# Softcap attention into a soft mixture of experts: queries and keys cast by transfers, and three exponential tiles per batch on VectorE rather than one

**Chip, cores, metric.** One Trainium2 chip, one core. The metric is device time of one execution in microseconds (us), median over runs. Executions of one kernel mostly agree within 0.3%; several kernels here, the old one among them, have now and then an execution about 2.5 us longer, which is told where it matters.

## The reference

```python
# q, k, v: (8 batches, 12 heads, 448 positions, 64); phi: (768, 32); w1: (8, 768, 1024); w2: (8, 1024, 768)
scores = q @ k.transpose(0, 1, 3, 2) / sqrt(64)
scores = cap * tanh(scores / cap)                  # cap = 30
attn = exp(scores - max) ; attn = attn / sum       # over keys
x = (attn @ v), heads put side by side             # (3584, 768)
logits = x @ phi
d = softmax of logits over the tokens ; slot_input = d.T @ x       # 8 experts x 4 slots
slot_out = relu(slot_input @ w1[e]) @ w2[e]
out = (softmax of logits over the slots) @ slot_out                # (3584, 768)
```

## The kernel before

Everything is scheduled by hand: the program fixes the order of each engine's instructions, and in the traces they run in that order (VectorE from 85.18 to 88.57 us of the changed kernel, below: key copy, last part of one tile, first part of the next, logit sum, as their slots put them). Attention works on 336 tiles of 128 x 448 scores, six to a **chunk**, so 56 chunks, seven to a batch of the input. "Chunk 2 of a batch" is one with number j%7 = 2. A **PV pass** multiplies the exponentials of two heads by their values on TensorE; VectorE then normalizes the result. The **logit sum** is the addition on VectorE that collects the logits of `x @ phi`. A **quad** is four heads, whose queries, keys or values are loaded together. PSUM holds the tiles that TensorE's matmuls and transposes write here (`space=PSUM` in the kernel). In the loop below each chunk has slots ("0", "a", "b", "c", "d") into which side work is hung with `at(chunk, slot, job)`.

```python
    exps = att.enter_context(tc.tile_pool(name="exps", bufs=4))   # four chunks of exponentials

    def tanh_chunk(i):                         # half a chunk: 3 tiles from PSUM, ScalarE
        j, half = divmod(i, CH // CS)
        if half == 0:
            exs[j] = exps.tile([P, CH, S], BF16, name="ex", tag="ex")
        # ... act.activation(exs[j][...], scores, ACT.Tanh, scale=...)

    def exp_chunk(j):                          # in place, ScalarE; tile 0 left out where VectorE does it
        exp_part(j, 1 if j in shared else 0, CH)

    shared = [j for j in range(NCH - 2) if j % 7 == 3 and j > 7] if cap < 80 else []

    def poly_exp(j, part):                     # one exponential tile on VectorE, in three parts
        t, bits = exs[j][:, 0, :], 2.0 ** 23
        if part == 0:    # three tensor_scalar: xe, xm, xe
            # ...
        elif part == 1:  # two scalar_tensor_tensor: xp <- xm ; xp <- xp, xm
            # ...
        else:            # two scalar_tensor_tensor: xp <- xp, xm ; t <- xp, xe
            # ...

    def cast(nm, Q):                           # a quad of heads, float32 -> bfloat16, VectorE
        t = cst.tile([P, NT, P], BF16, name=nm + "bf", tag=nm + "bf")
        dve.tensor_copy(t.rearrange("p c (h d) -> p h c d", h=2),
                        raws.pop((nm, Q)).rearrange("p h (c d) -> p h c d", d=DH))
        # ... then the load of the next quad

    def transp(nm, Q):                         # 7 transposes on TensorE, one copy on VectorE
        # ...
        for c in range(NT):
            pe.transpose(ps[:, c, :], src[:, c, :], ident)
        # ... dve.tensor_copy(t, ps)

    for j in range(NCH):                       # the loop; TensorE's order is the order of these lines
        run(j, "0")
        tanh_chunk(2 * j); tanh_chunk(2 * j + 1)
        # ... exp_chunk(j - 1)
        if pr is not None:
            pv_pass(pr, 0)                     # 14 matmuls, then norm(): reciprocal and xq on VectorE
        run(j, "a")
        qk_chunk(2 * j + 2)                    # scores of half of the next chunk
        run(j, "b")
        if pr is not None:
            pv_pass(pr, 1)
        run(j, "c")
        qk_chunk(2 * j + 3)
        run(j, "d")
```

Logit sums, transposes of attention output and of queries and keys share one bank of PSUM (tag "T"), so they follow each other in program order. The values are cast on GpSimd (`vcast`, two instructions per quad). `spare(n)` issues n matmuls without use, to keep TensorE busy.

The softmax here doesn't subtract the row's maximum and nothing guards it: scores larger than these inputs give would overflow.

## Time and profile before

| | before |
|---|---|
| median of the runs beside the changed kernel | 317.31 us (316.76 to 319.75, 4 runs) |
| span of the profiled run | 314.8 us |
| ScalarE / TensorE / VectorE / GpSimd busy | 89 / 86 / 62 / 34% |
| time from one batch to the next (start of the tanh of chunk 2 to the next such start) | 32.55 us, six times |
| last tanh of the attention | starts at 264.6 us; 50.3 us follow |

The lines of the page that carry these are in the prediction.

Waits of TensorE (engine, tile and line, what it waited for, us in total, times, longest):

```profile
PE sc L269 <- ACT ex L278: 7.9, 19, 0.7
PE qps L237 <- DVE lg L360: 2.7, 7, 0.4
```

TensorE waits for ScalarE (7.9 us), hardly for VectorE: the query transposes wait 0.4 us at most for the logit sum.

### The profile page before, as it was taken

The numbers are of one execution on the slowest core, as the hardware profiler recorded it, in microseconds if no ns is written. First come the engines' busy times: TensorE is split into PE (matmuls) and PEld (weight loads), VectorE is DVE, ScalarE is ACT, GpSimd is POOL, SyncE is SP. The second block draws the span as 40 slices with busy tenths as digits, with TensorE's granted clock in tenths as the row PEclk, the third lists the DMA queues.
The fourth block names the chain that finished last, engine by engine and source line by source line (L and its number), as shares of the span: only waits on it lengthen the run. The fifth ranks groups of instructions, "written<-read, shape, count | busy, mean of one in ns | idle before, by whom it ended". The sixth has DMA issues, their size and how long they took to land.

```text
span 314.8 us, 8844 instructions
## 1 busy us (share of the span) xinstructions
PE 269.4 (86%) x3804; PEld 191.0 (61%) x3804; DVE 193.7 (62%) x473; ACT 281.3 (89%) x208; POOL 106.5 (34%) x134
## 2 busy tenths in 40 slices
PE   7899898899889998898889989898889998998720
PEld 6667665667666665666666666666666677743400
DVE  3636565766586659575867587657766574327840
ACT  4999999999999999999999999999999999326730
POOL 2464342523543452354245416441732130200000
PEclk9999999999999999999999999999999999999985
DMA  8899999799999999999999999999999807898997
GB/s 223 267 234 238 291 244 269 159 231 256 235 210 231 266 237 207 254 220 266 194 225 269 221 264 190 242 235 266 209 232 254 214 14 207 290 393 301 389 411 314
DMA packets 57479, 77.68 MB, mean 247 GB/s; under 512 B 3809, under 2 KB 53601, under 8 KB 57441
## 3 DMA queue, kind: packets, MB, share of 16 engines
q0 software_dynamic: 30480, 25.22, 52.1%
q1 hardware_dynamic: 26672, 51.68, 48.1%
q8 instruction: 29, 0.48, 0.6%
q10 hardware_dynamic: 288, 0.23, 0.2%
q14 instruction: 10, 0.07, 0.1%
HBM read 91.32 MB, written 18.87 MB: 350 GB/s over the span
## 4 chain that ended last, share of the span: by engine, by line
ACT 67%; PE 20%; DVE 5%; issue 3%; DMA 2%; DVEq 0%; ACTq 0%
ACT ex L278 33%; ACT ex L282 32%; PE pv L318 5%; PE sc L269 3%; PE so_ps L676 2%; PE junk L506 2%; PE hp L649 2%; ACT ob L754 1%; PE op L702 1%; DMA kraw<-in_k_dram 1%; DVE xq L329 1%; PE op L745 1%; PE xps L344 1%; DMA out_dram<-obh 1%; DVE ob L752 1%
## 5 line engine op out<-in xcount | busy, mean ns | idle before, releaser
L278 ACT ACTIVATE ex<-sc 128x1344 bf16<-128x1344 f32 (+1 forms) x113 | 162.3, 1693 | 0.9 <-PE sc L269 0.8
L282 ACT ACTIVATE ex<-ex 128x2688 bf16<-128x2688 bf16 (+4 forms) x58 | 159.2, 2779 | 0.1
L318 PEld LDWEIGHTS <-ex 128*128 128x128 bf16 x1344 | 78.7, 97 | 21.5 <-DVE xq L329 17.8
L318 PE MATMUL pv<-vbd,ex 128*128 128x130 bf16 x1274 | 88.6, 220 | 2.6 <-ACT ex L282 0.7
L269 PE MATMUL sc<-qT,kT 64*64 64x448 bf16 x672 | 78.6, 358 | 8.2 <-ACT ex L278 7.9
L247 POOL CAST vbd<-vraw 64x896 bf16<-64x896 f32 x23 | 21.5, 936 | 103.6 <-PE pv L318 65.3
L269 PEld LDWEIGHTS <-kT 64*64 64x64 bf16 x672 | 27.3, 105 | 25.3 <-issue 7.5
L329 DVE TENSOR_TENSOR xq<-pv,rec 128x256 bf16<-128x256 f32 x91 | 38.6, 424 | 3.1
L328 DVE RECIPROCAL rec<-pv 128x4 f32<-128x4 f32 x91 | 16.5, 181 | 32.1 <-PE pv L318 31.2
L506 PEld LDWEIGHTS <-ones 128*128 128x128 bf16 x470 | 28.6, 100 | 11.6 <-DVE xq L329 8.0
L372 POOL COPY e<-E 128x512 bf16<-128x512 bf16 x9 | 7.2, 795 | 81.5 <-ACT E L366 49.6
L506 PE MATMUL junk<-ones 128*128 128x128 bf16 x433 | 31.4, 219 | 2.5 <-DVE xq L329 1.6
L239 DVE COPY kT<-kps 128x896 bf16<-128x896 bf16 x23 | 14.4, 625 | 24.6 <-PE kps L237 24.4
L109 POOL DMA_DIRECT2D w1b<-in_moe_w_dram x32 | 25.2, 791 | 0.0
L248 POOL CAST vbd<-vraw 64x896 bf16<-64x896 f32 x23 | 23.7, 1029 | 1.3
L346 DVE COPY xT<-xps 128x512 bf16<-128x512 bf16 x47 | 19.5, 415 | 3.2 <-PE xps L344 3.0
L344 PE MATMUL xps<-ident,xq 128*128 128x128 bf16 x188 | 18.1, 218 | 0.2 <-DVE zacc L383 0.2
L239 DVE COPY qT<-qps 128x896 bf16<-128x896 bf16 x23 | 14.2, 616 | 5.2 <-PE qps L237 5.2
L226 DVE CAST kbf<-kraw 128x896 bf16<-128x896 f32 x22 | 16.0, 728 | 1.3 <-DMA kraw<-in_k_dram 1.3
L237 PE MATMUL kps<-ident,kbf 128*128 128x128 bf16 x161 | 12.8, 219 | 4.2 <-DVE slacc L418 2.2
L237 PE MATMUL qps<-ident,qbf 128*128 128x128 bf16 x161 | 12.8, 219 | 3.2 <-DVE lg L360 2.7
L237 PEld LDWEIGHTS <-kbf 128*128 128x128 bf16 x161 | 10.0, 97 | 9.0 <-issue 8.3
(113 smaller groups left out, 255.5 us busy)
## 6 DMA issues: line engine op xcount, KB each, us to landing
w1b<-in_moe_w_dram POOLq DMA_DIRECT2D x32, 384.0 KB, 10.2
vraw<-in_v_dram SPq DMA_DIRECT2D x23, 448.0 KB, 6.6
qraw<-in_q_dram SPq DMA_DIRECT2D x22, 448.0 KB, 7.8
kraw<-in_k_dram SPq DMA_DIRECT2D x22, 448.0 KB, 6.0
w2d<-in_moe_w_dram POOLq DMA_DIRECT2D x20, 384.0 KB, 9.2
w2t<-w2d SPq DMA_DIRECT2D x20, 384.0 KB, 5.9
out_dram<-ob SPq DMA_DIRECT2D x8, 768.0 KB, 7.3
w2b<-in_moe_w_dram POOLq DMA_DIRECT2D x12, 384.0 KB, 9.9
```

The costliest lines, as they stand in the source:

```text
L109: pool.dma_start(out=w1b[e][:, js, fs], in_=w1r[:, e, js, fs])
L237: pe.transpose(ps[:, c, :], src[:, c, :], ident)
L239: dve.tensor_copy(t, ps)
L247: pool.tensor_copy(t[0:HP, :, :, 0:DH], raw[0:HP])
L248: pool.tensor_copy(t[HP:P, :, :, DH + 1:VW - 1], raw[HP:P])
L269: pe.matmul(sc[cs, u, 0:S], qkT["k", Q][r, c, cs], qkT["q", Q][r, :, cs], start=True, stop=True)
L278: act.activation(exs[j][:, half * CS + u0:half * CS + u1, :], sc[:, u0:u1, 0:S], ACT.Tanh, scale=qk_scale / cap)
L282: act.activation(exs[j][:, u0:u1, :], exs[j][:, u0:u1, :], ACT.Exp, scale=cap)
L318: pe.matmul(pvs[pr, half][:, n, 0:VW], exs[j][:, u, GOFF[g]:GOFF[g] + P], vbds[Q % 2][:, h, c, :], start=(c == 0 and n == 0), stop=(c == N ...
L329: dve.tensor_tensor(xq[Q][:, 2 * half:2 * half + 2, h * P:(h + 1) * P] .rearrange("p g (i d) -> p g i d", i=2), pv[:, :, :, 0:DH], rec.to_ ...
L344: pe.transpose(ps[:, g, :], xq[Q][:, g, h * P:(h + 1) * P], ident)
L506: pe.matmul(junk if home is None else home, ones, ones, start=True, stop=True)
```

## The change

Intent: ScalarE sets the pace, so give two more exponential tiles per batch to VectorE (chunks 1, 2 and 3 of a batch rather than 3 alone), and make room on VectorE by letting transfers do the casts of queries and keys. The keys and queries then lie head by head, so each transpose becomes a pair of 64-column ones; the keys of one quad are transposed a chunk earlier. The core of the diff:

```diff
-            sp.dma_start(out=t, in_=quad_ap(nm, Q))
+            (sp if nm == "v" else pool).dma_start(out=t, in_=quad_ap(nm, Q))   # bfloat16 tile: the transfer casts
...
         for c in range(NT):
-            pe.transpose(ps[:, c, :], src[:, c, :], ident)
+            for h in range(2):
+                pe.transpose(ps[h * HP:h * HP + HP, c, :], src[:, h, c * DH:(c + 1) * DH], ident)
...
-    shared = [j for j in range(NCH - 2) if j % 7 == 3 and j > 7] if cap < 80 else []
+    shared = [j for j in range(NCH - 2) if 1 <= j % 7 <= 3 and j > 7] if cap < 80 else []
...
-        quad_in(3 * b + 3, (j + 4, "a"), (j + 5, "a"), (j + 4, "d"), (j + 5, "c"),
+        quad_in(3 * b + 3, (j + 4, "a"), (j + 5, "a"), (j + 3, "d"), (j + 5, "c"),
...
-        at(j + 3, "d", spare, 10)
+        at(j + 3, "d", spare, 10 if b == 0 else 4)
...
-        for dj, slot, part in ((0, "a", 0), (0, "c", 1), (0, "d", 2)):
+        for part, (dj, slot) in enumerate((((0, "a"), (0, "c"), (1, "b")),
+                                           ((0, "c"), (0, "d"), (1, "a")),
+                                           ((0, "c"), (1, "a"), (1, "c")))[j % 7 - 1]):
             at(j + dj, slot, poly_exp, j, part)
```

Also in the diff: how the first two quads are still cast by engines, the slots in which the loads are issued, buffer bookkeeping, and the first output tile computed in two halves.

More of the change, by code (lines that the diff above doesn't have):

```diff
@@ L90 @@
     w1b = [wts.tile([P, NJ, F], BF16, name=f"w1b{e}", tag="w1", bufs=E)
-           for e in range(E - 1)]
+           for e in range(E - 2)]
     w2b = wts.tile([P, R2, D], BF16, name="w2b")
@@ L129 @@
     ld = att.enter_context(tc.tile_pool(name="ld", bufs=1))
-    cst = att.enter_context(tc.tile_pool(name="cst", bufs=1))
     ldv = att.enter_context(tc.tile_pool(name="ldv", bufs=1))
@@ L158, in raw_tile @@
     def raw_tile(nm):
-        return (ldv if nm == "v" else ld).tile([P, 2, S], F32, name=nm + "raw",
-                                               tag=nm + "raw")
+        if nm == "v":
+            return ldv.tile([P, 2, S], F32, name="vraw", tag="vraw")
+        return ld.tile([P, 2, S], BF16, name=nm + "b", tag=nm + "raw", bufs=2)
     def load(nm, Q):
@@ L164, in load @@
             t = raw_tile(nm)
-            sp.dma_start(out=t, in_=quad_ap(nm, Q))
+            (sp if nm == "v" else pool).dma_start(out=t, in_=quad_ap(nm, Q))
             raws[nm, Q] = t
     def load_first():
-        for nm in "qkv":
-            raws[nm, 0] = raw_tile(nm)
-        kc = raws["k", 0].rearrange("p h (c d) -> p h c d", d=DH)
+        for nm in "qk":
+            raws[nm, 0] = [ld.tile([P, S], F32, name=f"{nm}raw{h}", tag=nm + "raw", bufs=2)
+                           for h in range(2)]
+        raws["v", 0] = raw_tile("v")
+        kc = raws["k", 0][0].rearrange("p (c d) -> p c d", d=DH)
         kin = quad_ap("k", 0, 0).rearrange("p (c d) -> p c d", d=DH)
-        sp.dma_start(out=raws["q", 0][:, 0, :], in_=quad_ap("q", 0, 0))
+        sp.dma_start(out=raws["q", 0][0], in_=quad_ap("q", 0, 0))
         for c0, c1 in ((0, CS), (CS, NT)):
-            act.dma_start(out=kc[:, 0, c0:c1, :], in_=kin[:, c0:c1, :])
+            act.dma_start(out=kc[:, c0:c1, :], in_=kin[:, c0:c1, :])
         for nm in "kq":
-            sp.dma_start(out=raws[nm, 0][:, 1, :], in_=quad_ap(nm, 0, 1))
+            sp.dma_start(out=raws[nm, 0][1], in_=quad_ap(nm, 0, 1))
         t = wts.tile([P, 3, 2, S], F32, name="raw1", tag="w1", bufs=E)
+        t01 = wts.tile([P, 2, 2, NT, P], BF16, name="casts", tag="w1", bufs=E)
         for n, nm in enumerate("kqv"):
             raws[nm, 1] = t[:, n, :, :]
+            if nm != "v":
+                for Q in range(2):
+                    casts[nm, Q] = t01[:, n, Q, :, :]
             if nm == "v":
@@ L192, in first_pieces @@
                 copy(casts[nm, 0][:, c0:c1, cols],
-                     raws[nm, 0][:, h, c0 * DH:c1 * DH].rearrange("p (c d) -> p c d", d=DH))
+                     raws[nm, 0][h][:, c0 * DH:c1 * DH].rearrange("p (c d) -> p c d", d=DH))
             elif stage == "turn":
@@ L202, in first_half @@
             if h == 0:
-                casts[nm, 0] = cst.tile([P, NT, P], BF16, name=nm + "bf", tag=nm + "bf")
                 qkT[nm, 0] = qk.tile([P, NT, P], BF16, name=nm + "T", tag=nm + "T")
@@ L222, in first_half, with cast @@
                 load(nm, 2)
-    def cast(nm, Q):
-        t = cst.tile([P, NT, P], BF16, name=nm + "bf", tag=nm + "bf")
-        dve.tensor_copy(t.rearrange("p c (h d) -> p h c d", h=2),
-                        raws.pop((nm, Q)).rearrange("p h (c d) -> p h c d", d=DH))
-        casts[nm, Q] = t
-        if Q > 1:
-            load(nm, Q + 1)
+    def cast(nm):
+        dve.tensor_copy(casts[nm, 1].rearrange("p c (h d) -> p h c d", h=2),
+                        raws.pop((nm, 1)).rearrange("p h (c d) -> p h c d", d=DH))
     def transp(nm, Q):
-        src = casts.pop((nm, Q))
+        src = casts.pop((nm, Q)) if Q == 1 else raws.pop((nm, Q))
         home = (psV, "pv") if (nm, Q) == ("k", 1) else (psT, "T")
@@ L236, in transp @@
         for c in range(NT):
-            pe.transpose(ps[:, c, :], src[:, c, :], ident)
+            if Q == 1:
+                pe.transpose(ps[:, c, :], src[:, c, :], ident)
+                continue
+            for h in range(2):
+                pe.transpose(ps[h * HP:h * HP + HP, c, :], src[:, h, c * DH:(c + 1) * DH], ident)
         t = qk.tile([P, NT, P], BF16, name=nm + "T", tag=nm + "T")
@@ L441, in quad_in @@
         if 0 < Q < NQ:
-            at(*cast_k, cast, "k", Q)
-            at(*cast_q, cast, "q", Q)
+            for nm, when in (("k", cast_k), ("q", cast_q)):
+                at(*when, *((cast, nm) if Q == 1 else (load, nm, Q + 1)))
             at(*k_in, transp, "k", Q)
@@ L453 @@
             quad_in(3 * b + 1, (j - 1, "b"), (j, "a"), (j - 1, "d"), (j, "c"), (j + 1, "d"))
-        quad_in(3 * b + 2, (j + 1, "c"), (j + 2, "c"), (j + 2, "b"), (j + 2, "d"),
+        quad_in(3 * b + 2, (j, "d"), (j + 1, "c"), (j + 2, "b"), (j + 2, "d"),
                 (j + 4, "d"))
-        quad_in(3 * b + 3, (j + 4, "a"), (j + 5, "a"), (j + 4, "d"), (j + 5, "c"),
+        quad_in(3 * b + 3, (j + 4, "a"), (j + 5, "a"), (j + 3, "d"), (j + 5, "c"),
                 (j + 6, "d"))
@@ L701, in half_tile @@
         bb, c = divmod(n, NT)
+        if n == half == 0:
+            for p, (bank_p, mul) in enumerate(zip(home, (act.mul, dve.tensor_scalar_mul))):
+                cs = slice(p * HD // 2, (p + 1) * HD // 2)
+                pe.matmul(bank_p, et_tile(bb, c), so[half][:, cs], start=True, stop=True)
+                mul(ob[:, cs], bank_p, winv[:, bb, c:c + 1])
+            store(n, half, half + 1, ob)
+            return
         pe.matmul(home, et_tile(bb, c), so[half], start=True, stop=True)
@@ L721 @@
             for eng in ("act", "dve"):
-                half_tile(done, 0, bank([P, HD], name="op0"), eng)
+                half_tile(done, 0, bank([P, HD], name="op0") if done else
+                          [bank([P, HD // 2], name="op00") for _ in range(2)], eng)
                 done += 1
```

## The prediction

> **What bounds the kernel now.** I read the page's busy line and chain first, to name the limiting engine; then the chain in order of time, to price one tile; then the same chain in a late window, to see who stands right behind the limit; then busy times by chunk.
>
> ```profile
> PE 269.4 (86%) x3804; PEld 191.0 (61%) x3804; DVE 193.7 (62%) x473; ACT 281.3 (89%) x208; POOL 106.5 (34%) x134
> ACT 67%; PE 20%; DVE 5%; issue 3%; DMA 2%; DVEq 0%; ACTq 0%
> L278 ACT ACTIVATE ex<-sc 128x1344 bf16<-128x1344 f32 (+1 forms) x113 | 162.3, 1693 | 0.9 <-PE sc L269 0.8
> L282 ACT ACTIVATE ex<-ex 128x2688 bf16<-128x2688 bf16 (+4 forms) x58 | 159.2, 2779 | 0.1
> ```
>
> ScalarE is busy 89% of the span, has two thirds of the chain, and its tanh (L278) and exponential (L282) have 1.0 us of idle time ahead of them in all. From 6.8 to 266 us, the attention stage, it practically never waits. The rest, some 49 us, is layers and stores. The chain in order of time gives its beat:
>
> ```profile
> 52.02 2.36 ACT ex L278 x2
> 54.38 2.33 ACT ex L282
> 56.91 2.36 ACT ex L278 x2
> 59.27 1.96 ACT ex L282
> ```
>
> A chunk is 2.36 us of tanh and 2.33 us of exponential, 4.69 us. Where VectorE already takes one tile of six (chunk 10, whose exponential runs during chunk 11) the exponential is 1.96 us: **0.37 us saved per tile**. But the same view of 214 to 246 us leaves ScalarE at 216.6 and does not come back for a whole batch. It starts like this:
>
> ```profile
> 217.40 0.92 PE pv L318 x14
> ...
> 218.56 0.42 DVE xq L329
> 218.99 0.54 DVE xp L300
> ...
> 219.55 0.64 DVE xp L301
> ...
> 220.22 0.64 DVE xp L303
> ...
> 220.87 0.92 DVE ex L304
> ...
> 221.91 0.43 DVE xq L329
> ...
> 222.40 0.97 PE pv L318 x14
> ```
>
> The reader is to see that the one exponential tile on VectorE already stands on the chain: the second normalization (221.91) waits behind its four multiply-adds, and TensorE's next PV pass (222.40) waits for that normalization. TensorE and VectorE together form a second loop, nearly as long as ScalarE's. The busy times by chunk (chunks 16 to 19, columns PE, PEld, DVE, ACT, POOL) say why:
>
> ```profile
> 80.00:84.70 4.70, 3.84 (x57) 2.80 (x55) 2.15 (x4) 4.70 (x5) 3.47 (x5) 1.00 0.90 242
> 84.70:89.59 4.89, 4.32 (x62) 3.19 (x60) 4.17 (x11) 4.89 (x5) 0.00 (x0) 1.00 1.14 220
> 89.59:93.91 4.32, 3.63 (x63) 2.54 (x61) 3.46 (x9) 4.32 (x4) 2.71 (x4) 1.00 1.13 189
> 93.91:98.65 4.74, 4.32 (x58) 3.23 (x58) 3.46 (x9) 4.74 (x4) 3.19 (x4) 1.00 0.95 240
> ```
>
> In chunk 17, which has that tile, VectorE is busy 4.17 of 4.89 us. Chunk 16 is light, for it has no PV pass.
>
> [...] the last multiply-add (L304) takes 627 ns once and 911 to 915 six times, a GpSimd copy or cast beside it where I looked, and a cast of 0.62 us becomes 0.98 beside one. [...] The trace shows the kinds equally fast per source byte: 50.4 MB of weights, cast, took 52.1% of the engines, and 51.7 MB uncast took 48.1%. [...]
>
> **The change, part by part.**
> 1. *Exponential tiles.* The rule goes from j%7 = 3 (7 tiles) to 1, 2, 3 (21). 14 more leave ScalarE: 14 x 0.37 = **5.2 us off the path**, if all else keeps up. On VectorE a tile is 0.38+0.39+0.39+0.61+0.63+0.63+0.63 = 3.7 us without contention (groups by form), 14 x 3.7 = +52 us.
> 2. *Casts.* 44 of 46 whole-quad casts leave VectorE: 16.0+14.5 = -30.5 us. Net +21 us of 193.7; per batch of 32.7 us from 22.1 to about 25.5. It fits on average.
> 3. *Transposes.* 22 quads x 2 x 7 become pairs of 64-column ones, 308 more matmuls; 42 filler matmuls go (six per batch), and the instruction count agrees with both. 64-column transposes of one half took 0.55 us for 7 (at 7.85 us), as do whole ones. [...] I take 95 ns per pair against 79 (between fully side by side and in turn): 6 x 7 x 16 ns = +0.7 us per batch, less 6 fillers x 73 ns = 0.4. About nothing.
> 4. *GpSimd.* 44 more issues of 0.79 us, and it is 34% busy: off the path.
> 5. *Tail.* The first output tile is halved between two engines, so the first store goes some 0.2 us sooner.
> All of it at full worth: 317.2 - 5.2 - 0.2 = 311.8 us.
>
> **Where it may be given back.** The order of instructions puts the new parts on VectorE like this, from chunk 16 on: key copy, last part of tile 1, first part of tile 2, *logit sum*, query copy, second part of tile 2, *normalization*, and so on. TensorE must have the logit sum before it transposes the queries (one PSUM bank for both), and the PV pass of chunk 17 stands behind these transposes. With starts to starts from the timeline (key copy 0.54, last part 1.21, first part 1.18): key copy at 82.7 as before, logit sum at 85.6 instead of 83.95, query transposes at 86.0 instead of 84.30, PV at 86.6 instead of 84.69: 1.9 us later. The middle part (1.23) then delays the normalization to 88.5, the second PV pass to 89.2 instead of 86.62, and the second half of the scores to 90.7. ScalarE at its new pace asks for that half at 80.00 + 2 x 4.32 + 0.20 (the small exponential of the logits) + 1.18 = 90.0. So it stalls 0.7 us, and two tiles saved 0.74: a first batch breaks even here. Carried on in the same way through chunks 17 to 22, the next batch's first scores come 34.5 us after this batch's, against 32.7 now (81.24 to 113.97).
>
> **Rivals.**
> *A, ScalarE still sets the pace.* For it: casts leave the busiest time of VectorE, chunks 5, 6 and 0 of a batch get lighter, the parts are placed in the chunk without PV, and the scores are 2.2 to 2.9 us ahead of ScalarE in chunks 15 to 17. Gives 312 to 315.
> *B, the loop of TensorE and VectorE takes over.* For it: the late chain and the working above. At 1.8 us for each of six batches after the first, about +10 us: 327; with 0.5 us per batch instead, 320. Against it: some fifty steps, each uncertain by 0.03 us.
> *C, the keys and queries land late.* GpSimd is in order, so a load stands behind a value cast that waits for PV (65 us of such waits, up to 6.6 each).
>
> ```profile
> w1b<-in_moe_w_dram POOLq DMA_DIRECT2D x32, 384.0 KB, 10.2
> qraw<-in_q_dram SPq DMA_DIRECT2D x22, 448.0 KB, 7.8
> ```
>
> A GpSimd transfer lands after 10.2 us. The tightest load by my count, queries issued after the cast of 70 to 72 us and wanted in the slot at 84, has 11 us. It should just do; where it does not, some tenths per batch go. [...] 319 to 324.
>
> **Range and chances.** The floor is 311.8, so over 2% faster (310.9) needs a gain that I do not see: 0.05. I give A 0.4, centred on 313.5, and B and C together 0.6, centred near 324, since the loop was already at its limit before. The weighted mean is 0.4 x 313.5 + 0.6 x 324 = 319.8; I say **319.5 us**, range **312 to 330**. Slower by over 2% means above 323.6, somewhat over half of B and C: 0.35. Within 2%: 0.60.
>
> **What would show it.** Right for part 1: 21 exponentials of five tiles at 1.96 us in the chain, and L282 some 5 us less busy. Right for the casts: no whole-quad cast after quad 1, and VectorE some 20 us busier. For B: ScalarE waits for scores (0.8 us now) for several us in all, once or more per batch in chunks 3 to 5, the chain in the middle of the run passes through PV, normalization and polynomial, and the query copy waits some 2 us more per batch. For C: the transposes of keys or queries wait for a DMA. For A: ScalarE's waits stay under 2 us. I am wrong in the working if the normalization behind a polynomial part does not hold up PV, or if ScalarE waits although VectorE has idle time just there; wrong in the size if the 64-column transposes take turns, which would show as 14 of them in over 1 us.

## More of the kernel before

The slices of the page show TensorE's granted clock, each digit a fortieth of the span, 9 for (nearly) full.

```profile
PEclk9999999999999999999999999999999999999985
```

## The result, and the profile after

The changed kernel takes **345.64 us** (345.37 to 345.79, 4 runs) against 317.31 in the same rounds. The ratio is 1.0876, 95% interval 1.0819 to 1.0932. It is slower, and outside the predicted range. The page of the changed kernel (busy line, granted clock, chain by engine):

```profile
PE 286.1 (83%) x4071; PEld 198.2 (58%) x4071; DVE 222.5 (65%) x528; ACT 278.7 (81%) x208; POOL 139.7 (41%) x178
PEclk9999998999999978999999989995999859999965
PE 45%; DVE 33%; ACT 13%; DMA 3%; issue 2%; DVEq 0%; SPq 0%; ACTq 0%
```

Two things are to be seen. ScalarE's share of the chain fell from 67% to 13%, and VectorE's rose from 5% to 33%: the limit has changed hands. And TensorE's granted clock, full before, dips in several slices. (The dip in the last slices, the stores, was there before; the others are new.) The waits of the changed kernel:

```profile
ACT ex L286 <- PE pv L326: 26.0, 17, 3.6
PE qps L245 <- DVE lg L368: 13.5, 7, 1.9
PE pv L326 <- DVE ex L312: 8.3, 7, 1.3
```

ScalarE, which waited 0.8 us, now waits 26.0 us for the PV pass (a tanh needs one of the four buffers of exponentials, which a PV pass frees). TensorE waits 13.5 us for the logit sum, once per batch 1.9 us, where it was 2.7 us in all, and 8.3 us for the last polynomial part. The chain in order of time, in the middle of the run (start, length, what), shows where these waits come from:

```profile
84.63 0.53 PE kps L245 x14
...
85.18 0.62 DVE kT L247
85.81 0.55 DVE xp L311
86.37 0.64 DVE ex L312
...
87.11 0.40 DVE xe L302
...
87.96 0.40 DVE xe L306
88.36 0.21 DVE lg L368
...
88.61 0.60 PE qps L245 x14
...
97.74 0.80 DVE xp L311
...
98.57 1.26 DVE ex L312
...
99.88 0.52 PE pv L326 x6
```

Between the key copy and the logit sum stand the last part of tile 1 (L311, L312) and the first part of tile 2 (L302 to L306). TensorE, which must have that sum, transposes queries only at 88.61. Except for these transposes (until 89.23) VectorE is on the chain without a gap until 99.83, where the last part of tile 3 ends and a PV pass can go on. The timeline of the same stretch (start, length, engine, line, what, how often, and the idle time before it with its releaser):

```profile
88.61 0.58 PE L245 MATMUL qps<-ident,qb 128*64 128x128 bf16 x14 [1.94 <-DVE lg L368]
...
90.03 0.76 PE L277 MATMUL sc<-qT,kT 64*64 64x448 bf16 x6
...
91.65 0.98 PE L326 MATMUL pv<-vbd,ex 128*128 128x130 bf16 x14 [0.87 <-DVE xq L337]
...
92.55 2.47 ACT L286 ACTIVATE ex<-sc 128x1344 bf16<-128x1344 f32 x2 [1.85 <-PE pv L326]
```

TensorE stands still for 1.94 us, the second PV pass starts at 91.65, and ScalarE, ready at 90.70, starts the tanh at 92.55, though its scores had been there from 90.79.

**Where 29.2 us of span went** (314.8 to 344.0), from the starts of the tanh of chunk 2 in the traces, and the run with fillers below (e4), which has the change at full clock:

| part | before | with fillers, full clock | changed | 
|---|---|---|---|
| batch to batch, mean of six | 32.55 | 34.96 | 35.87 |
| chunk 2 of the last batch starts | 242.45 | 257.13 | 262.43 |
| from there to the last tanh | 22.10 | 25.62 | 28.75 |
| after the start of the last tanh | 50.28 | 52.86 | 52.81 |
| span | 314.84 | 335.60 | 343.99 |

So with the clock at full: 14.7 us in the batches before, 3.5 in the last one, 2.6 after it, 20.8 in all; the other 8.4 are the clock. (The profiled run before is one of its shortest, so the medians of the times differ by 28.3 rather than 29.2.)

The granted clock can be read directly in windows of 8 us (window, length, then busy us and instructions of PE, PEld, DVE, ACT, POOL, then the granted clock, the share of the DMA engines and GB/s). The changed kernel:

```profile
264.00:272.00 8.00, 6.01 (x102) 4.52 (x100) 5.72 (x12) 7.48 (x6) 1.72 (x3) 1.00 0.66 161
272.00:280.00 8.00, 7.25 (x57) 5.04 (x56) 4.75 (x12) 4.43 (x3) 0.79 (x1) 0.50 0.01 2
```

From 272 to 280 us TensorE runs at half clock: 57 matmuls keep it busy for 7.25 us, where 102 took 6.01 just before. The clock's records in the trace have six such stretches:

```text
start us   length us   granted clock
 53.62       3.41        0.5
125.30       6.83        0.5
196.97       3.41        0.5
231.11      10.24        0.5
272.07      10.24        0.5
330.10      15.91        0.5    (the stores; before: from 304.12)
```

The first five start after or in the 1.93 to 1.94 us in which TensorE waits for the logit sum (51.4, 121.9, 194.3, 229.6 and 268.6 us); after the same wait at 86.7 and 158.9 the clock stayed. Before the change TensorE had one idle stretch of over 0.7 us before 299 us, of 0.75 us. A single wait of that length wasn't needed: in e5 below the clock halved seven times before 335 us, and no idle stretch of TensorE up to there was over 1.37 us. And e4 kept its clock through the attention with stretches of up to 1.30 us. So the length of one wait did not decide it here; what did was not looked into.

### The profile page after: what moved, and what is told of

It is laid out like the page before. It is cut to its first block, busy times and chain, and to the rows that moved or that the text cites. A ratio compares the mean times of both kernels' runs of the same rounds, so it can differ in the third digit from the quotient of the medians. Undisturbed runs are those within 1.5% of the kernel's fastest.

```text
span 344.0 us, 9411 instructions
## 1 busy us (share of the span) xinstructions
PE 286.1 (83%) x4071; PEld 198.2 (58%) x4071; DVE 222.5 (65%) x528; ACT 278.7 (81%) x208; POOL 139.7 (41%) x178
## 4 chain that ended last, share of the span: by engine, by line
PE 45%; DVE 33%; ACT 13%; DMA 3%; issue 2%; DVEq 0%; SPq 0%; ACTq 0%
PE pv L326 16%; PE sc L277 9%; ACT ex L286 7%; DVE xq L337 6%; ACT ex L290 5%; DVE ex L312 4%; PE junk L516 4%; DVE xp L311 3%; DVE qT L247 3%; PE kps L245 3%; DVE xp L309 2%; DVE rec L336 2%; DMA out_dram<-ob 2%; PE xps L352 2%; DVE xm L304 2%
## 5 line engine op out<-in xcount | busy, mean ns | idle before, releaser
L286 ACT ACTIVATE ex<-sc 128x1344 bf16<-128x1344 f32 (+1 forms) x113 | 140.0, 1291 | 28.8 <-PE pv L326 26.0
L290 ACT ACTIVATE ex<-ex 128x2688 bf16<-128x2688 bf16 (+4 forms) x58 | 130.0, 2246 | 0.1
L326 PE MATMUL pv<-vbd,ex 128*128 128x130 bf16 x1274 | 96.7, 230 | 13.3 <-DVE ex L312 8.3
L326 PEld LDWEIGHTS <-ex 128*128 128x128 bf16 x1344 | 84.1, 102 | 37.5 <-DVE xq L337 20.3
L277 PE MATMUL sc<-qT,kT 64*64 64x448 bf16 x672 | 83.1, 376 | 1.5 <-ACT ex L286 1.2
L255 POOL CAST vbd<-vraw 64x896 bf16<-64x896 f32 x23 | 22.6, 983 | 104.6 <-PE pv L326 88.8
L256 POOL CAST vbd<-vraw 64x896 bf16<-64x896 f32 x23 | 25.9, 1126 | 1.3
L245 PE MATMUL qps<-ident,qb 128*64 128x128 bf16 x308 | 13.4, 228 | 13.6 <-DVE lg L368 13.5
L245 PEld LDWEIGHTS <-qb 128*64 128x64 bf16 x308 | 10.5, 112 | 15.4 <-issue 13.7
L352 PE MATMUL xps<-ident,xq 128*128 128x128 bf16 x188 | 18.6, 222 | 0.8 <-DVE kT L247 0.3
L309 DVE SCALAR_TENSOR_TENSOR xp<-xp,xm 128x448 f32<-128x448 f32 x21 | 18.4, 876 | 0.7
L312 DVE SCALAR_TENSOR_TENSOR ex<-xp,xe 128x448 bf16<-128x448 f32 x21 | 17.5, 835 | 0.7
```

The source lines that it names most:

```text
L245: pe.transpose(ps[h * HP:h * HP + HP, c, :], src[:, h, c * DH:(c + 1) * DH], ident)
L256: pool.tensor_copy(t[HP:P, :, :, DH + 1:VW - 1], raw[HP:P])
L277: pe.matmul(sc[cs, u, 0:S], qkT["k", Q][r, c, cs], qkT["q", Q][r, :, cs], start=True, stop=True)
L286: act.activation(exs[j][:, half * CS + u0:half * CS + u1, :], sc[:, u0:u1, 0:S], ACT.Tanh, scale=qk_scale / cap)
L290: act.activation(exs[j][:, u0:u1, :], exs[j][:, u0:u1, :], ACT.Exp, scale=cap)
L309: dve.scalar_tensor_tensor(xp, xp, POW2[2], xm, ALU.add, ALU.mult)
```

## The experiments

Each was compared with the kernel before in the same rounds. "Batches" are the six times from batch to batch as above. Theory: the loop of TensorE and VectorE sets the time, because of the amount of VectorE work put into chunks 1 to 3, and the clock adds to it. Rivals: late transfers, the order of the parts, GpSimd's casts slowing VectorE, the number of buffers.

### Casts by transfers alone, one tile (e1)

```diff
-    shared = [j for j in range(NCH - 2) if 1 <= j % 7 <= 3 and j > 7]
+    shared = [j for j in range(NCH - 2) if j % 7 in (3,) and j > 7]
     # and its parts in the old slots: (0, "a"), (0, "c"), (0, "d")
```

> The changed kernel with one exponential tile per batch on VectorE, in the chunk and the slots of the kernel before; everything else of the change stays (casts by transfers, paired transposes, key transposes sooner, fillers, tail). Theory 1 (the added VectorE work lengthens the loop of TensorE and VectorE): VectorE has some 4 us per batch less than in the kernel before, so ScalarE sets the pace again: 315 to 318 us, a batch takes 32.5 us as before, and the TensorE clock never falls in the attention stage. Theory 2 (loads and casts on GpSimd, or the doubled transposes, cost the time): it stays above 330 us, and transposes wait for DMAs.

Measured: 318.29 us (318.03 to 320.85), before 317.61; ratio 1.0037 (0.9972 to 1.0103). Batches 32.55, as before, clock full (0.976 to 0.982 over the runs, with the stores; before 0.98 to 0.986). So, while ScalarE sets the pace, neither the transfers nor GpSimd's issues nor the paired transposes cost anything that can be told from noise, and taking 28 us from VectorE (193.7 to 165.4 us busy) gains nothing by itself, since ScalarE still sets the pace. The transfers on the GpSimd queue of the changed kernel even landed sooner than weights, which are larger, did before (10.2 us for 384 KB; KB each, us from issue to landing):

```profile
qb<-in_q_dram POOLq DMA_DIRECT2D x22, 224.0 KB, 6.2
kb<-in_k_dram POOLq DMA_DIRECT2D x22, 224.0 KB, 7.7
```

and no transpose of keys or queries waited for a DMA, in e1 or in the changed kernel. The late loads of rival C are out.

### Three tiles without the new casts (e2)

```diff
     # the kernel before, with the three tiles per batch and the slots of the change
-    shared = [j for j in range(NCH - 2) if j % 7 == 3 and j > 7]
+    shared = [j for j in range(NCH - 2) if 1 <= j % 7 <= 3 and j > 7]
```

> The kernel before with the three tiles in the changed kernel's slots; queries and keys are still cast on VectorE. If VectorE's load in chunks 1 to 4 sets the loop, the casts that stay there (two key casts and one or two query casts of 0.62 us among them) make it longer than in the changed kernel: batches of 35.5 to 37 us and 346 to 360 us. If casts by transfers did not help the loop: 343 to 346 us.

Measured: 370.8 us (2 runs), ratio 1.1689; batches 37.61 to 41.13; mean clock 0.905 and 0.896 in the two runs; ScalarE waits 51.4 us for PV. More than expected. With three tiles the casts by transfers, with the rest of the change (key transposes a chunk earlier, fewer fillers), are worth 25 us; with one tile they are worth nothing. Here the worth of this part went with which engine set the pace.

### Two tiles (e9 and e8)

```diff
     # e9: tiles of chunks 1 and 3 in the slots of the change
-    shared = [... if 1 <= j % 7 <= 3 and j > 7]
+    shared = [... if j % 7 in (1, 3) and j > 7]
     # e8: the same tiles, tile 1 at (1, "a"), (1, "c"), (1, "d"), tile 3 in the old slots
```

> The changed kernel without its second tile: chunks 1 and 3 of a batch keep theirs, in the changed kernel's slots. If the amount of VectorE work sets the loop: 3.7 us less VectorE work between the key copy and the last part, so batches come to 32.2 to 33.5 us, the wait for the logit sum shrinks by 1.2 us to under 1 us, the clock stays full, and the whole is 316 to 324 us. If any tile next to the logit sum breaks it: batches stay above 34 us, above 335 us.

> Two tiles per batch: that of chunk 1 wholly in chunk 2, which has no PV pass (its last part behind the logit sum and the query copy), that of chunk 3 in the slots of the kernel before. If the loop of TensorE and VectorE has room there: batches of 32.2 us (32.55 less 0.37), 315.5 to 316.5 us. If it has none: batches of 32.6 us and more, 318 us and up.

Measured: e9 322.91 us (2 runs), ratio 1.0155, batches 32.18 to 33.37, clock full (0.98 over the profiled run), 4.0 us of waits for the logit sum. e8 325.56 us (4 runs), ratio 1.0254, batches 33.08 to 33.93: the PV pass waits for the tile's last part (7.8 us, 7 times), so those slots are too late, and the worse branch of the expectation came true. (Two of its four runs were 3 us longer at a clock of 0.959 rather than 0.98.) In the slots of the change one tile less takes the mean batch from 34.96 at full clock (e4) to 32.84 (e9), so the amount of work matters, and not in proportion: the slack is used up first. But it isn't the amount alone. The same two tiles in the slots of e10 below take 32.17, and in e8's 33.30.

### Fillers in TensorE's wait (e4)

```diff
+        if b:
+            at(j + 2, "d", spare, 22)          # 22 matmuls without use ahead of the query transposes
         quad_in(3 * b + 2, (j, "d"), (j + 1, "c"), (j + 2, "b"), (j + 2, "d"),
```

> The changed kernel with 22 filler matmuls (1.6 us) put where TensorE waits 1.9 us for the logit sum, in each of the seven batches. Theory 1b (these idle stretches halve TensorE's clock for 3.4 to 10.2 us, which stretches the batches of 37.6, 35.9 and 37.7 us): the clock stays at full until the stores, every batch takes 34.6 to 34.9 us, and the whole is 335 to 338 us. Rival (the low clock falls where TensorE waits for VectorE anyway): 344 to 347 us.

Measured: 337.34 us (336.55 to 337.43, 4 runs), ratio 1.0604. The granted clock of its page:

```profile
PEclk9999999999999999999999999999999999999975
```

The batches take 34.59, 34.62, 35.53, 34.86, 35.52 and 34.61 us. The second and the fourth, in which the changed kernel kept its clock too, took 34.65 and 34.87 there, so the fillers lie in idle time. (The first took 34.57 in spite of 3.4 us at half clock.) The clock is thus worth 345.64 - 337.34 = **8.3 us**, shown by adding work and nothing else. Two of the six took 0.9 us longer at full clock. The timeline shows 0.6 of it: in these batches the sums for the output weights (`e_sums`, every second batch) stand ahead of the logit sum in chunk 1, and all that follows on VectorE comes 0.60 us later. The rest stays open.

### GpSimd's value casts made tiny (e3, e7)

```diff
-        pool.tensor_copy(t[0:HP, :, :, 0:DH], raw[0:HP])
+        pool.tensor_copy(t[0:HP, :, 0:1, 0:1], raw[0:HP, :, 0:1, 0:1])
     # likewise the other half; the result is wrong on purpose
     # e7: the same and the fillers of e4
```

In the changed kernel's timeline the same two multiply-adds are seen beside GpSimd's cast and without it:

```profile
82.45 1.23 POOL L256 CAST vbd<-vraw 64x896 bf16<-64x896 f32 x1
...
82.90 1.26 DVE L309 SCALAR_TENSOR_TENSOR xp<-xp,xm 128x448 f32<-128x448 f32 x1
...
90.42 0.63 DVE L309 SCALAR_TENSOR_TENSOR xp<-xp,xm 128x448 f32<-128x448 f32 x1
```

1.26 us rather than 0.63. Such long ones come about once per batch at each of the four multiply-adds (0.80, 1.26, 0.80 to 1.00 and 1.25 us, rather than 0.62), some 1.7 us per batch.

> The changed kernel, but GpSimd's two value casts per quad write one column each; the result is wrong on purpose. Theory 1a (VectorE's two-input polynomial parts wait for GpSimd's casts, and that is on the path): the parts that take 0.80, 1.26, 0.88 and 1.25 us beside a value cast go back to 0.62, 1.7 us per batch, 7 batches: some 12 us less, 332 to 335 us, more if the clock recovers too. Rival (the contention lies where VectorE has slack): within 3 us of 345.6.

> The changed kernel with the 22 fillers and with the tiny value casts (wrong on purpose), so that the contention is measured at a steady clock. If VectorE's wait for GpSimd's casts is on the path: batches of 33.7 us, as those of the tiny-cast run that kept their clock, instead of 34.6 to 35.5 in the run with fillers alone, and 329 to 332 us. If the casts cost nothing on the path: 336 to 338 us.

Measured: e3 342.39 us (2 runs), ratio 1.0768: all but four of the 84 parts were back at 0.61 to 0.63 us and the undisturbed batches at 33.71, but the clock dropped in more batches (0.86 to 0.95 in four of six; 0.929 and 0.912 over the two runs), so the total missed its expectation and says nothing on the size. e7, with the clock held but for 3.4 us in the last batch, tells it: 331.84 us (2 runs), ratio 1.0436, batches 33.74 to 34.76, mean 34.14. Against e4 that is **5.5 us**, and 0.82 per batch: half of the 1.7 us summed from the durations reach the time. The trace shows where. Chunk 3 is as slow as in e4 (6.66 and 6.67 us), but chunks 5 and 6 take 4.69 and 4.67 rather than 5.04 and 5.07: the last part of tile 3 no longer stands beside a cast (0.62 + 0.63 us rather than 0.88 + 1.26), and the PV pass that waits for it starts sooner.

### Parts moved behind the logit sum and the query copy (e5)

```diff
-        (((0, "a"), (0, "c"), (1, "b")), ((0, "c"), (0, "d"), (1, "a")), ((0, "c"), (1, "a"), (1, "c")))
+        (((0, "a"), (0, "c"), (1, "d")), ((0, "d"), (1, "a"), (1, "c")), ((0, "d"), (1, "a"), (1, "c")))
```

> The changed kernel with the last part of tile 1 and the first part of tile 2 moved behind the logit sum and the query copy, and the first part of tile 3 behind the key copy. If the order is the fault (TensorE waits for the logit sum): the wait of 1.9 us goes, the clock stays up, and the batches come down to 33 us or less: below 332 us. If the amount is the fault (VectorE is busy without a gap from the key copy to the last part of tile 3, 14.7 us, in whatever order): the wait moves to the normalizations, batches still take 34 to 35 us, and the whole is 335 to 345 us, by the clock.

Measured: 353.47 us (2 runs), ratio 1.1117, batches 35.1 to 42.32 with a clock of 0.80 to 0.95 in several (0.919 and 0.928 over the two runs), worse than either branch expected. Its waits:

```profile
PE pv L326 <- DVE ex L312: 16.9, 14, 1.3
PE pv L326 <- DVE xq L337: 9.7, 11, 1.4
...
PE qps L245 <- DVE lg L368: 2.7, 7, 0.4
```

The wait for the logit sum is gone (0.4 us at most, as before the change), and what was gained came back as waits of the PV pass for the polynomial's last part, twice those of the changed kernel. So it is not this one place in the order that is wrong: the work does not fit in that stretch in the orders tried.

### A fifth buffer of exponentials (e15, e16, e17)

ScalarE's 26 us of waits name the PV pass, which frees a buffer of exponentials. That can be the cause or a sign. A fifth buffer needs room, so four more blocks of second-layer weights go by way of DRAM; e16 is the control with that alone; e17 has the fillers too.

```diff
-    exps = att.enter_context(tc.tile_pool(name="exps", bufs=4))
+    exps = att.enter_context(tc.tile_pool(name="exps", bufs=5))   # e15, e17
-    R2 = 24
+    R2 = 20                                                       # e15, e16, e17
```

> The changed kernel with five buffers of exponentials rather than four; the room comes from four rows of second-layer weights less held in memory (they go by way of DRAM like the others). If the buffer is the limit (rival), ScalarE no longer waits for the PV pass, a batch loses most of its 1.85 us stall and takes 33 us or so, and the time falls by 8 us or more, under 338. If the loop of TensorE and VectorE is the limit (theory), the wait of ScalarE goes to the scores instead, by 0.7 us shorter at most since the second half of the scores stands behind the same PV pass, the normal batch stays at 34.2 to 34.7 us and the time at 342 to 347, with the clock dropping as before.

> The control of the run before: four buffers, but the second-layer weights moved in the same way. All theories: as the changed kernel, 344 to 348, with waits of ScalarE for the PV pass of about 26 us in all; what it differs by from the changed kernel is the price of the weights moved.

> The changed kernel with the 22 fillers in TensorE's wait for the logit sum, which kept the clock at full (337.3 us, batches of 34.6), and five buffers of exponentials. Theory (loop of TensorE and VectorE): full clock, batches of 34.2 to 34.7, 335 to 339. Rival (buffer): batches of 33 and under 332.

Measured: e15 350.07 us (346.73 to 352.25, 4 runs, the longest slow; the three fast ones have a median of 349.0), e16 348.05 (346.49 to 349.3), e17 340.31 (339.76 to 340.44), e4 337.34. The totals of e15 and e17 lie above their expectations mostly because of the part after the last tanh, which grew from 52.8 us to 54.0 with the weights moved (e16) and to 56.7 and 56.6 with five buffers too (e15, e17). The batches decide: in e17 34.60, 34.64, 35.54, 34.86, 35.53, 34.63, the same within 0.03 us as in e4 with four buffers. The waits of e4, then of e17:

```profile
ACT ex L286 <- PE pv L326: 17.4, 15, 3.0
```

```profile
ACT ex L286 <- PE sc L277: 16.9, 20, 1.3
```

The wait went from the buffer to the scores and kept its size. The buffer is a sign; the lateness of TensorE behind VectorE is the cause, as the runs with a tile less (e9) and without contention (e7) agree. Here the list of waits named what came last (a PV pass in e4, the scores in e17), not what was scarce.

### A better version? (e10, e12, e13)

```diff
-    shared = [... if 1 <= j % 7 <= 3 and j > 7]
+    shared = [... if j % 7 in (1, 3) and j > 7]
     # e10: tile 1 at (0, "a"), (0, "c"), (1, "a"), so with its last part ahead of the key copy;
     #      tile 3 in the old slots; first output tile whole again
     # e12: as e10, but tile 1 at (0, "c"), (1, "a"), (1, "a")
     # e13: e10 and an unused tile of 3.5 KB where the cast tiles were
```

> Two tiles per batch, with the last part of chunk 1's tile ahead of the key copy, where VectorE waits 1.5 us for the key transposes, and chunk 3's tile as in the kernel before; the first store whole. If what matters is that no part stands between key copy, logit sum and query copy, nor ahead of a PV pass that needs it: batches of 32.2 us, ScalarE waits under 1 us, 314.5 to 316 us. If any second tile is too much for the loop: batches of 32.8 us or more, 319 us and up.

> As the run with the early last part, but the first part comes after chunk 1's second normalization and both others ahead of the key copy in chunk 2. If the gap there holds 2.4 us of VectorE work: as the former, 314.5 to 316 us; if not, the key copy and the logit sum come about 0.8 us later than in the former, 316 to 319 us.

> The run with two tiles and the early last part, with the unused pad tile, to see whether two tiles beat both kernels. If the attention stage is shortened for good (262.6 us at its last tanh, against 264.6) and the tail's difference is chance: 315 to 316 us, ratio 0.993 to 0.997. If the tail takes it back: 317.3 to 318, ratio about 1.000.

Measured: e10 317.74 us (315.86 to 319.37, 4 runs: two near 316, two near 319), ratio 1.0027, which misses the expected 314.5 to 316. Its batches are 32.17 us all six, 0.38 less than before, with full clock (0.982 over the profiled run) and no wait of ScalarE for PV or scores on the list: the second tile's 0.37 us per batch arrive whole. Chain of its page:

```profile
ACT 59%; PE 23%; DVE 9%; DMA 2%; issue 2%; DVEq 0%; ACTq 0%; SPq 0%
```

ScalarE leads again. But 51.9 us follow the last tanh rather than 50.3, which takes back 1.6 of the 1.9 us gained by then. e12: 331.03 us (4 runs), ratio 1.0458, batches 32.61 to 36.03, clock down to 0.86 (0.926 to 0.95 over the runs): with the second and third part together ahead of the key copy there isn't room for them, a miss. e13: 316.2 us (315.43 to 318.85, 6 runs) against 317.42, ratio 0.9947 (0.9892 to 1.0002). That is the best version found, some 0.5% faster and not told apart from before with certainty. Its profiled run was one of the longer kind, like that of e3: in both traces chunk 2 starts at 18.6 us rather than 16.5 to 17.0, and in e13's the first record of TensorE's clock, of full, is at 13.6 us, rather than at 5.8 as in the changed kernel's.

### The part after the attention (e6, e11, e14)

```diff
+    pad = att.enter_context(tc.tile_pool(name="pad", bufs=1))      # e6: e1 and this unused tile
+    pad.tile([P, NT, 2 * P], BF16, name="pad")
     # e11: e6 and the first output tile whole again
     # e14: the kernel before, unchanged
```

> The kernel with one tile and casts by transfers, plus an unused 3.5 KB tile in the place of the two cast tiles that the change removed, so that the second-layer weights find memory that is free before the attention stage ends. If the missing early load costs the tail 1.5 us: the second weight load starts by 250 us instead of 258, and the whole is 316.3 to 317.2 us. If not: as without it, 318.0 to 318.6 us.

> One tile, casts by transfers, the unused pad tile, and the first output tile whole as in the kernel before. If the halving of the first tile is what costs the tail some 1.5 us: 316.3 to 317.0 us. If it does nothing or gains its intended 0.2 us: 318.0 to 318.4 us.

> The kernel before once more, for a second profile of it. Its first profile ends 50.2 us after the last tanh starts; every variant, that with vector casts and the old tail among them, ends 51.5 to 52.9 us after it. If this is chance from run to run: the second profile has 51.5 us or more as well, or the runs of the one program spread over 316.5 to 320. If it belongs to the kernels: 50.2 us again.

Measured: e6 318.03 us, 52.1 us after the last tanh; e11 318.18 us, 52.0; e14 317.29 us (316.73 to 319.71), 50.5. So the shorter tail belongs to the kernel before and is not chance; it comes neither from where its buffers lie (e6 moved the second-layer loads earlier, as meant, to no avail) nor from the halved first tile. e2, which has the old casts and old tail but another rhythm, had 52.0 as well. **What makes the tail 1.2 to 2.6 us longer in the variants stays open.**

## Why the prediction was wrong

- **ScalarE's beat: right.** An exponential of five tiles takes 2.07 to 2.10 us in the changed kernel's timeline, one of six 2.44 to 2.47: 0.37 per tile. e10 shows it in the time.
- **Casts and transposes: right.** Casting transfers and paired transposes cost nothing (e1). 14 paired 64-column transposes take 0.58 us in the timeline (88.61 above), where the 7 whole ones took 0.55 to 0.56; estimated 95 ns per pair, measured 83. VectorE got 28.8 us busier (193.7 to 222.5) rather than some 20. The halved first output tile gained nothing that can be seen (52.1 us after the last tanh in e6, 52.0 with the tile whole in e11).
- **Rival C: wrong** on the loads, refuted by e1. It was a reason for weight near 319 to 324. Contention with GpSimd was real, on VectorE's side (0.8 us per batch, e7).
- **Rival B's mechanism: right, and its loop too.** It put the logit sum ahead of query transposes, PV, normalization and second PV, and gave 34.5 us per batch. The batches undisturbed by the clock took 34.65 and 34.87. The changed kernel's chunk 16 starts 2.1 us later than before (timelines: 81.76, 79.69), so its 86.0 for the query transposes becomes 88.1 (measured 88.6), and 89.2 for the second PV pass becomes 91.3 (91.65). The size agrees partly by chance: without GpSimd in the way the loop is 33.75 (e7), so the working had steps that were too long, and it left out 0.8 us of contention.
- **The step that failed first: "a first batch breaks even here."** It compared a stall of 0.7 us with 0.74 saved, for one stall, and stopped at the next chunk. It forecast six long batches and a free first one. The first batch with the tiles took 34.57 us, 2.0 more than before. The stall was 1.85 us: the working let the first tanh of chunk 18 start and had only the second one wait for its scores, but the first already waits for a buffer that the second PV pass frees. The means by chunk of the traces (start of a chunk's tanh to the next, chunks 0 to 6 of a batch) show why:

| | 0 | 1 | 2 | 3 | 4 | 5 | 6 | sum |
|---|---|---|---|---|---|---|---|---|
| before | 4.67 | 4.68 | 4.68 | 4.87 | 4.30 | 4.68 | 4.68 | 32.56 |
| e4, change at full clock | 4.67 | 4.75 | 4.30 | 6.67 | 4.46 | 5.04 | 5.07 | 34.96 |

  Only the tile in chunk 1's exponential (chunk 2, -0.38) is seen as a gain. Chunk 3 loses 1.80 after its own 0.37 is taken off, where the working had 0.7 before that (the stall shown above was 1.85 us). Chunks 5 and 6 lose 0.75 more. That is the contention with GpSimd's casts, for it is gone in e7, whose chunk 3 is as late: TensorE's PV pass waits up to 1.3 us for tile 3's last part, which is long beside a cast. The last batch has all of its late chunks too and pays in full (25.6 us rather than 22.1 to the last tanh).
- **The term that was missing: TensorE's clock, 8.3 us (e4).** The working delayed TensorE by 1.9 us per batch and did not ask what that does to the granted clock (0.93 over the profiled run of the changed kernel, 0.982 over that of e4 with the waits filled), although the kernel is full of matmuls without use, six of which per batch the change took away.
- **The sum.** Rival B had 1.8 us for each of six batches, 10.8 (rounded to 10 there: 317.2 and 10.8 make 328, not 327). Of the spans' 29.2 us, measured at full clock, the batches took 14.7 (+3.9); not forecast were the last batch with 3.5, the tail with 2.6 and the clock with 8.4.
- **The weighing.** A got 0.4, though the step-by-step working, the only argument with numbers for this stretch, had given 34.5 us per batch. Averaging 313.5 with 324 gave a number that neither stood for; B and C "centred near 324" already cut B's own 327.
- Of the signs named: five-tile exponentials, no whole-quad casts, ScalarE's waits and the chain through PV, normalization and polynomial came as named for B. The waits were foretold as waits for scores; they named the PV pass, and e17 showed that it makes no difference. The query copy waited hardly longer in all (6.0 us rather than 5.2); the 2 us were TensorE's wait ahead of it. "L282 some 5 us less busy" can't be used: the sum fell from 159.2 to 130.0 us, but that of the tanh, whose work stayed the same, fell from 162.3 to 140.0 as well, so the lengths of these records can't be compared.

## What to carry to other kernels

Before moving work off the limiting engine, find which loop of other engines is the next limit and how much slack it has in the very stretch that receives the work; the engine's average share (62% here) said nothing of it, and a second tile in slots that had room gained its 0.37 us per batch (e10), while in the slots of the change the third one cost some 2 us per batch (e9, e4). The waits added to TensorE cost twice here, by their length (1.93 to 1.94 us per batch) and by the clock granted afterwards (8.3 us in all); 22 matmuls without use in the gap kept the clock up (e4). Where a wait names a buffer, another buffer is the test of whether the buffer matters.
